# A three-part kernel on one core: weight conversions in other steps of the MLP loop, and four small copies earlier

## The chip, the cores and the metric

The kernel runs on one core of a Trainium2 chip. The metric is the time of one execution on the device in microseconds (us), lower being better. The times are medians over repeated runs; the profile is of one execution.

## What is computed

Attention with two kinds of mask, a soft mixture of experts, and an MLP, one after the other. The change lies in the MLP and its input:

```python
c = logits - logits.max(1, keepdims=True)      # 2304 tokens x 32 slots
c = np.exp(c)
c /= c.sum(1, keepdims=True) + 1e-09
x = c @ slot_out                               # 2304 x 512
h = np.maximum(x @ w_in, 0.0)                  # w_in 512 x 2048
out = h * h @ w_out                            # w_out 2048 x 512
```

All weights arrive as 64-bit floats.

## The kernel before

Attention and experts take the first 200 us. The MLP never forms `x`. It computes A = slot_out @ w_in in quarters of 512 columns (`a_chunk`, line 1090), and h as c @ A.

**The loop.** The 2048 hidden columns are taken in NC = 4 quarters c, the tokens in NSB = 3 blocks of 768, and the 4 pieces of 128 hidden columns of a quarter are the innermost loop (QF = 4). That makes 48 steps n, 12 for each quarter, and j is the step's number in its quarter. A step multiplies one piece of h (768 tokens x 128) by one 128 x 512 piece of w_out: 18 matmuls on PE (line 1205), three for each of six token tiles t, into six PSUM banks, named `s`, `s`, `o`, `o`, `t1`, `t1`. The three are high part of h by high part of the weight, low part of h by high, high by low: the third one needs the weight's low half.

After four steps (j = 3, 7, 11) the banks are full and are emptied into `part`: in the first quarter by copies, one bank on ACT and the next on DVE (line 1218), in the others by additions on DVE alone (line 1220). In the last quarter each result is sent out.

**h.** `emit_h` (line 1155) makes half a piece of h, some one and a half steps ahead: one PE matmul (line 1165) into a bank `t2`, relu and square on ACT (1173, 1174), rounding to the high part on ACT (1175), the low part by a subtraction on DVE (1180). It is called twice in a step, at t = 1 and t = 4.

**Conversions.** `conv_late` (1084) takes the next loaded weight piece and makes 32-bit values of it (`narrow`, 178): one instruction on POOL (line 189, into `nm`), then three on DVE (192, 193, 196, the last into `wi` for w_in or `wf` for w_out). For w_out two more follow one step later in `conv_split` (at t = 1): a rounding on ACT to the high half (1081) and a subtraction on POOL to the low half (1082). The order is fixed: w_out 0 to 3, then for each of quarters 1, 2 and 3 four pieces of w_in and four of w_out. Each conversion frees the buffer of its 64-bit piece, and `fetch` issues the next load into it on SP's queue. Two w_out pieces are converted ahead of the loop, the rest at t = 4 of a step, where the line of the diff allows it: before, steps 0 to 9 of the first quarter, and j = 2 to 9 of the second and third.

**Combine weights.** c (2304 x 32) is kept as high and low part. `c_parts` (978) copies the two parts of one of the four batches side by side (POOL, lines 981 and 982, tile `c4`, two buffers), and `c_transpose` (984) transposes them on PE (line 990) into `cT4`, the moving operand of line 1165. Batches 0 and 1 are copied during the experts, three groups of transposes run ahead of the loop, and five behind steps 0, 1, 3, 4 and 5 (`TR`).

**Order.** The program order of each of the four compute engines is pinned as the code emits it; an engine takes its instructions in that order, and each waits for what it needs.

Of the kernel before, what the change touches and what calls it, by code (L numbers as in the profile page):

```python
# [31 lines left out]
def kernel(  # L32
# [49 lines left out]
    def behind(ins, other):  # L82

        tc.add_manual_dep(
            ins.ins, other.ins.name,
            mybir.DependencyInfo(mybir.DependencyClass.NoSync, mybir.DependencyReason.DATA),
            reason="issue order",
        )
# [32 lines left out]
    def psum(tag):  # L121
        if tag == "t":
            tag = ("t1", "t1", "t2", "t2")[nt[0] % 4]
            nt[0] += 1
        return pp.tile([128, 512], F32, tag=tag, name=tag, bufs=2)


    def fill(n, ins):
        ps = psum("s")
        for _ in range(n):  # L130
            new = nc.tensor.matmul(
                out=ps[:, 0:256], lhsT=identb, rhs=fillb, start=True, stop=True
            )
            behind(new, ins)
            ins = new
# [821 lines left out]
    def c_softmax():  # L957
        cm = tail.tile([128, NTT], F32, name="cm")
        ch = tail.tile([128, NTT, 32], F32R, name="ch")
        behind(nc.vector.tensor_reduce(out=cm, in_=cl_, axis=AX.X, op=ALU.max), sT_ready)  # L960
        nc.vector.tensor_tensor(
            out=cl_, in0=cl_, in1=cm[:, :, None].to_broadcast([128, NTT, 32]), op=ALU.subtract
        )
        nc.scalar.activation(out=cl_, in_=cl_, func=AF.Exp)
        nc.vector.tensor_reduce(out=cm, in_=cl_, axis=AX.X, op=ALU.add)
        nc.vector.tensor_scalar(out=cm, in0=cm, scalar1=1e-9, scalar2=None, op0=ALU.add)
        nc.vector.reciprocal(out=cm, in_=cm)
        nc.vector.tensor_tensor(
            out=cl_, in0=cl_, in1=cm[:, :, None].to_broadcast([128, NTT, 32]), op=ALU.mult
        )  # L970
        nc.scalar.copy(out=ch, in_=cl_)
        chf = ch.bitcast(F32)
        nc.vector.tensor_tensor(out=cl_, in0=cl_, in1=chf, op=ALU.subtract)
        return chf
# [3 lines left out]
    def c_parts(chf, b):  # L978

        c4 = c4s[b] = tail.tile([128, 5, 2, 32], F32, tag="c4", name="c4", bufs=2)  # L980
        nc.gpsimd.tensor_copy(c4[:, :, 0, :], chf[:, 5 * b:5 * b + 5, :])
        nc.gpsimd.tensor_copy(c4[:, :, 1, :], cl_[:, 5 * b:5 * b + 5, :])

    def c_transpose(b, t0, t1, after=None):
        c4 = c4s[b]
        ps = psum("t2")
        n = min(t1 * 128, S) - t0 * 128
        for t in range(t0, t1):
            nr = min(128, S - t * 128)
            ins = nc.tensor.transpose(  # L990
                out=ps[0:64, ts(t - t0, 128)][:, 0:nr], in_=c4[0:nr, t].rearrange("p a s -> p (a s)"),
                identity=ident[0:nr, 0:nr],
            )
            if after is not None:
                behind(ins, after)
            after = None
        c0 = b * S + t0 * 128
        for i in range(2):
            (nc.vector.tensor_copy if i else nc.scalar.copy)(out=cT4[ts(i, 64), c0:c0 + n], in_=ps[0:64, 0:n])
        return ins  # L1000
# [76 lines left out]
    def conv_split():  # L1077
        while split:
            t, r = split.pop(0)
            hi, lo = t[:, 0:512], t[:, 512:1024]  # L1080
            nc.scalar.copy(out=hi, in_=r)  # L1081
            nc.gpsimd.tensor_tensor(out=lo, in0=r, in1=hi.bitcast(F32), op=ALU.subtract)  # L1082

    def conv_late(early=False):
        if todo or early:
            (conv_in if todo[0][0] == "in" else lambda: conv_out(early))()
            fetch()


    def a_chunk(c, tag, n0=0, n1=2):  # L1090
        two = tag == "o"
        pss = [psum(tag)[:, 0:(n1 - n0) * 128] for _ in range(1 + two)]
        for n in range(n0, n1):
            for kt in range(KD):
                for i in range(2):
                    ins = nc.tensor.matmul(
                        out=pss[i * two][ts(i, 64), ts(n - n0, 128)],
                        lhsT=soT[:, kt].rearrange("p a s -> p (a s)"),
                        rhs=wi[c][kt][:, ts(2 * n + i, 128)],
                        start=(kt == 0), stop=(kt == KD - 1), tile_position=(0, 64 * i),  # L1100
                    )
        if c == 0 and n0 == 0:
            fill(6, ins)
        if n0 == 0:
            A4[c] = mp.tile([128, 512], F32R, tag="A4", name="A4", bufs=2)
        cv = A4[c].rearrange("p (s i w) -> p i s w", i=2, w=128)[:, :, n0:n1]
        pv = [p.rearrange("p (s w) -> p s w", w=128) for p in pss]
        for i in range(2):
            nc.scalar.copy(out=cv[0:64, i], in_=pv[i * two][ts(i, 64)])
        for i in range(2):  # L1110
            nc.vector.tensor_tensor(
                out=cv[64:128, i], in0=pv[i * two][ts(i, 64)], in1=cv[0:64, i].bitcast(F32), op=ALU.subtract
            )

    CP = [(b, t0, t1) for b in range(B) for t0, t1 in ((0, 3), (3, 5))]
    for layer, pr in order:
# [5 lines left out]
        if (layer, pr) == (2, 0):  # L1122
            chf = c_softmax()
# [13 lines left out]
    A4 = {}  # L1137
    conv_split()
    a_chunk(0, "o", 0, 1)


    TB = 6
# [2 lines left out]
    QF = KF // NC  # L1145
    seq = [(c, sb, QF * c + j) for c in range(NC) for sb in range(NSB) for j in range(QF)]
    gs = {}

    TR = (0, 1, 3, 4, 5)


    halves = [(n, i) for n in range(len(seq)) for i in range(2)]
# [2 lines left out]
    def emit_h():  # L1155
        if not halves:
            return
        n, i = halves.pop()
        c, sb, f = seq[n]
        if i == 0:  # L1160
            gs[n] = slot(F32R), slot(F32R)
        gh, gl = (x[:, ts(i, HB)] for x in gs[n])
        ps = psum("t2")
        c0 = sb * 2 * HB + i * HB
        nc.tensor.matmul(  # L1165
            out=ps[:, 0:HB], lhsT=A4[c][:, ts(f % QF, 128)], rhs=cT4[:, c0:c0 + HB], start=True, stop=True
        )
        r = mp.tile([128, HB], F32, tag="r", name="r", bufs=3)
        if n == 0 and i:
            nc.vector.tensor_scalar(out=r, in0=ps[:, 0:HB], scalar1=0.0, scalar2=None, op0=ALU.max)  # L1170
            nc.vector.tensor_tensor(out=r, in0=r, in1=r, op=ALU.mult)
        else:
            nc.scalar.activation(out=r, in_=ps[:, 0:HB], func=AF.Relu)  # L1173
            nc.scalar.activation(out=r, in_=r, func=AF.Square)  # L1174
        nc.scalar.copy(out=gh, in_=r)  # L1175
        lows.append((gl, r, gh))
        if n or i:
            while lows:
                gl, r, gh = lows.pop(0)
                nc.vector.tensor_tensor(out=gl, in0=r, in1=gh.bitcast(F32), op=ALU.subtract)  # L1180
# [8 lines left out]
    for n, (c, sb, f) in enumerate(seq):  # L1189
        gh, gl = gs.pop(n)  # L1190
        first, last = f % QF == 0, f % QF == QF - 1
        j = n % (NSB * QF)
        if first:
            acc = [psum(a) for a in ("s", "s", "o", "o", "t1", "t1")]
        for t in range(TB):
            if t == 1:
                emit_h()
                conv_split()
            elif t == 4:
                emit_h()  # L1200

                if n < QF - 2 or QF - 2 <= j < 3 * QF - 2:
                    conv_late()
            for k, (a, w) in enumerate(((gh, 0), (gl, 0), (gh, 1))):
                nc.tensor.matmul(  # L1205
                    out=acc[t], lhsT=a[:, ts(t, 128)], rhs=wo[f][:, ts(w, 512)],
                    start=(first and k == 0), stop=(last and k == 2),
                )
            if not last:
                continue  # L1210

            r = sb * TB + t
            pt = part[:, r]
            nh = 2 if n == len(seq) - 1 and t == TB - 1 else 1
            for i in range(nh):
                cs = ts(i, 512 // nh)
                if c == 0:
                    (nc.vector.tensor_copy if t % 2 else nc.scalar.copy)(out=pt, in_=acc[t])
                else:
                    nc.vector.tensor_tensor(out=pt[:, cs], in0=acc[t][:, cs], in1=pt[:, cs], op=ALU.add)  # L1220
                if c == NC - 1:
                    nc.sync.dma_start(out=out[128 * r:128 * r + 128, cs], in_=pt[:, cs])
        if j == 3 * QF - 4 and c < NC - 1:
            a_chunk(c + 1, "t2")
        if n in TR:
            x = CP[3 + TR.index(n)]
            if x[1] == 0:
                c_parts(chf, x[0])
            c_transpose(*x)
    pin()  # L1230


# [28 lines left out]
```

## Time and profile before

| | |
|---|---|
| median of 3 runs | 446.71 us (443.96 to 447.89) |
| span of the profiled execution | 439.8 us |
| PE busy (matmul) | 411.3 us, 94% |
| DVE, ACT, POOL busy | 260.4, 282.3, 63.4 us |
| MLP loop on PE, first to last matmul | 203.2 us to 435.3 us |
| HBM read, written | 64.55 MB, 4.72 MB |

The span is the time from the first to the last instruction of the profiled execution; no time of that execution beside its span is shown, and the median of the runs is 6.9 us above it. The profile gives for each engine its instructions with start and duration, and for idle time what ended it.

### The profile page before, as it was taken

To read this page: it belongs to the slowest core of one execution; us is meant where nothing else is said; L and a number is where in the kernel's file an instruction comes from. 1 tells how busy PE (TensorE), PEld (TensorE's weight loads), DVE (VectorE), ACT (ScalarE), POOL (GpSimd) and SP (SyncE) were. 2 spreads that over 40 slices of the span, in tenths; PEclk is the share of its full clock that TensorE was granted. 3 is DMA by queue.
4 is the path that set the end of the run, shared out by engine and by line. 5 is a ranking of instruction groups with operands and counts; after the bars stand their busy time and mean duration, and the time that the engine had idled before them with its cause. 6 is when DMAs were issued, how large, how long until landed. Compare 5 with 4: busy or idle time off the path is not lost.

```text
span 439.8 us, 8657 instructions
## 1 busy us (share of the span) xinstructions
PE 411.3 (94%) x3310; PEld 305.6 (69%) x3310; DVE 260.4 (59%) x577; ACT 282.3 (64%) x583; POOL 63.4 (14%) x91
## 2 busy tenths in 40 slices
PE   8987988999989899979799999999999999999995
PEld 5665665766757644446578788877888787888884
DVE  7485665765766651036676754678664777725444
ACT  5977667887767411016686787657666676766660
POOL 7211001010110001002440340012320113100000
PEclk9998989999989969999999999999999999999999
DMA  9998939769957889998233211412000000003033
GB/s 193 284 280 246 253 93 302 219 195 281 323 165 230 283 309 371 386 401 327 95 95 97 97 43 54 136 56 95 1 1 1 0 0 2 0 1 144 24 121 144
DMA packets 38889, 69.83 MB, mean 159 GB/s; under 512 B 12736, under 2 KB 19136, under 8 KB 38848
## 3 DMA queue, kind: packets, MB, share of 16 engines
q1 hardware_dynamic: 38848, 69.28, 50.3%
q8 instruction: 26, 0.43, 0.4%
q14 instruction: 15, 0.12, 0.1%
HBM read 64.55 MB, written 4.72 MB: 158 GB/s over the span
## 4 chain that ended last, share of the span: by engine, by line
PE 67%; ACT 12%; DVE 10%; issue 5%; DMA 3%; POOL 1%; SPq 0%; DVEq 0%; ACTq 0%; POOLq 0%
PE t L1205 12%; PE s L1205 12%; PE o L1205 11%; PE s L532 4%; PE o L1010 4%; ACT space L471 3%; ACT space L477 3%; PE s L508 3%; PE t L452 3%; PE t L1037 3%; DVE part L1220 3%; PE t L1165 3%; DMA w<-in_moe_w_in_dram 2%; PE o L613 2%; DVE nm L193 2%
## 5 line engine op out<-in xcount | busy, mean ns | idle before, releaser
L1180 DVE TENSOR_TENSOR w<-r,w 128x384 fp32r<-128x384 f32 x96 | 57.8, 606 | 82.5 <-ACT w L1175 82.2
L1205 PE MATMUL s<-w 128*128 128x512 f32 x288 | 83.0, 396 | 0.5 <-POOL w L1082 0.5
L1205 PE MATMUL t<-w 128*128 128x512 f32 x288 | 75.1, 395 | 3.6 <-DVE part L1220 3.5
L1173 ACT ACTIVATE r<-t 128x384 f32<-128x384 f32 x95 | 46.7, 491 | 46.1 <-PE t L1165 38.7
L1205 PE MATMUL o<-w 128*128 128x512 f32 x288 | 73.7, 391 | 0.0
L1205 PEld LDWEIGHTS t<-w 128*128 128x128 f32 x288 | 53.0, 188 | 15.6 <-DVE part L1220 5.0
L1205 PEld LDWEIGHTS o<-w 128*128 128x128 f32 x288 | 54.0, 188 | 12.4
L1205 PEld LDWEIGHTS s<-w 128*128 128x128 f32 x288 | 52.7, 188 | 11.3 <-POOL w L1082 0.9
L1174 ACT ACTIVATE r<-r 128x384 f32<-128x384 f32 x95 | 50.0, 526 | 3.0
L1175 ACT CAST w<-r 128x384 fp32r<-128x384 f32 x96 | 49.2, 514 | 3.3
L471 ACT COPY space<-t 64x288 f32<-64x288 f32 x62 | 38.0, 614 | 11.7 <-PE t L452 10.3
L452 PE MATMUL t<-ident,space 96*128 96x96 f32 x192 | 29.7, 283 | 3.9 <-ACT space L477 2.3
L189 POOL TENSOR_SCALAR nm<-w 128x512 f32<-128x512 f32 x28 | 20.0, 720 | 90.5 <-DVE w L196 35.2
L1082 POOL TENSOR_TENSOR w<-wf,w 128x512 fp32r<-128x512 f32 x16 | 21.2, 1325 | 78.6 <-ACT w L1081 78.6
L1165 PE MATMUL t<-cT,A 128*128 128x384 f32 x96 | 32.2, 337 | 0.0
L477 ACT ACTIVATE space<-t 64x288 f32<-64x288 f32 (+1 forms) x46 | 29.0, 642 | 3.2 <-PE t L452 2.1
L452 PEld LDWEIGHTS t<-ident,space 96*128 96x128 f32 x192 | 20.6, 157 | 12.3 <-issue 3.9
L551 POOL TENSOR_TENSOR space<-space,sm 128x576 f32<-128x576 f32 x7 | 8.3, 1191 | 100.7 <-DVE sm L550 29.9
L193 DVE SCALAR_TENSOR_TENSOR nm<-w,nm 128x512 uint32<-128x512 uint32 x32 | 22.1, 692 | 1.0
L532 PE MATMUL s<-space 128*36 128x72 f32 x256 | 22.2, 317 | 0.0
L485 DVE TENSOR_REDUCE mx<-s 128x8 f32<-128x288 f32 (+2 forms) x32 | 14.9, 469 | 12.3 <-PE s L532 6.8
L1165 PEld LDWEIGHTS t<-cT,A 128*128 128x128 f32 x96 | 17.9, 188 | 4.4 <-ACT r L1173 0.5
(189 smaller groups left out, 564.5 us busy)
## 6 DMA issues: line engine op xcount, KB each, us to landing
w<-in_moe_w_dram SPq DMA_DIRECT2D x47, 512.0 KB
space<-in_moe_w_dram SPq DMA_DIRECT2D x17, 512.0 KB
w<-in_moe_w_in_dram SPq DMA_DIRECT2D x16, 512.0 KB
w<-in_moe_w_out_dram SPq DMA_DIRECT2D x16, 512.0 KB
space<-in_k_dram SPq DMA_DIRECT2D x16, 288.0 KB
space<-in_q_dram SPq DMA_DIRECT2D x16, 288.0 KB
out_dram<-part SPq DMA_DIRECT2D x17, 256.0 KB
space<-in_v_dram SPq DMA_DIRECT2D x16, 144.0 KB
```

The source lines that it names most:

```text
L193: nc.vector.scalar_tensor_tensor(out=r, in0=hi, scalar=0x80000000, in1=r, op0=ALU.bitwise_and, op1=ALU.bitwise_or)
L452: nc.tensor.transpose(out=pv[:, r, :], in_=src[:, h, 2 * r:2 * r + 2, :], identity=ident[0:96, 0:96])
L471: ins = (nc.vector.tensor_copy if dve else nc.scalar.copy)(out=o, in_=i)
L477: nc.scalar.activation(out=o, in_=i, func=AF.Copy, scale=scale)
L532: nc.tensor.matmul(out=ps[64 * h:64 * h + 36, ts(r, 72)].rearrange("p (a w) -> p a w", a=2), lhsT=qv[:, h, 4 * g + r, :], rhs=kv[:, :, h, ...
L1082: nc.gpsimd.tensor_tensor(out=lo, in0=r, in1=hi.bitcast(F32), op=ALU.subtract)
L1165: nc.tensor.matmul(out=ps[:, 0:HB], lhsT=A4[c][:, ts(f % QF, 128)], rhs=cT4[:, c0:c0 + HB], start=True, stop=True)
L1173: nc.scalar.activation(out=r, in_=ps[:, 0:HB], func=AF.Relu)
L1174: nc.scalar.activation(out=r, in_=r, func=AF.Square)
L1175: nc.scalar.copy(out=gh, in_=r)
L1180: nc.vector.tensor_tensor(out=gl, in0=r, in1=gh.bitcast(F32), op=ALU.subtract)
L1205: nc.tensor.matmul(out=acc[t], lhsT=a[:, ts(t, 128)], rhs=wo[f][:, ts(w, 512)], start=(first and k == 0), stop=(last and k == 2),)
```

## The change

Two edits, both in the MLP. The table `CONV` takes the place of the range j = 2 to 9: conversions now run in steps j = 1, 2, 4, 5, 6, 8, 9, 10 of a quarter (and still in steps 0 and 1), not in 3, 7 and 11, the steps that empty the banks. There are eight places in a quarter as before, but the first quarter now has 9 and had 10, so that the last piece of each later group moves to j = 1 of the next quarter. And the copies of batch 2 are issued right behind the first `a_chunk` ahead of the loop instead of behind step 1; those of batch 3 behind step 1 instead of behind step 4.

```diff
@@ -1137,6 +1137,7 @@
     A4 = {}
     conv_split()
     a_chunk(0, "o", 0, 1)
+    c_parts(chf, 2)
@@ -1147,6 +1148,7 @@
     TR = (0, 1, 3, 4, 5)
+    CONV = [j for j in range(1, 3 * QF - 1) if j % QF != QF - 1]
@@ -1199,7 +1201,7 @@
             elif t == 4:
                 emit_h()
 
-                if n < QF - 2 or QF - 2 <= j < 3 * QF - 2:
+                if n < QF - 2 or j in CONV:
                     conv_late()
@@ -1223,10 +1225,9 @@
         if n in TR:
-            x = CP[3 + TR.index(n)]
-            if x[1] == 0:
-                c_parts(chf, x[0])
-            c_transpose(*x)
+            c_transpose(*CP[3 + TR.index(n)])
+            if n == 1:
+                c_parts(chf, 3)
     pin()
```

Two lines are added ahead of the loop's body, so its line numbers rise by two (1205 becomes 1207, 1220 becomes 1222).

DVE's order around step 15, which empties the banks of the second quarter's first block, before. `part` with an `s`, `o` or `t1` bank is an addition, `w<-r,w` is the low part of h, and lines 192, 193 and 196 are one conversion:

```order
L196 SCALAR_TENSOR_TENSOR wi_3393<-w_2841,nm_3394 128x512
L1220 TENSOR_TENSOR part_2622<-s_3291,part_2622 128x512
L1180 TENSOR_TENSOR w_3385<-r_3413,w_3384 128x384
L1220 TENSOR_TENSOR part_2622<-s_3292,part_2622 128x512
L1220 TENSOR_TENSOR part_2622<-o_3293,part_2622 128x512
L1220 TENSOR_TENSOR part_2622<-o_3294,part_2622 128x512
L1180 TENSOR_TENSOR w_3431<-r_3434,w_3430 128x384
L192 TENSOR_SCALAR nm_3439<-nm_3439 128x512
L193 SCALAR_TENSOR_TENSOR nm_3439<-w_2886,nm_3439 128x512
L196 SCALAR_TENSOR_TENSOR wi_3393<-w_2886,nm_3439 128x512
L1220 TENSOR_TENSOR part_2622<-t1_3295,part_2622 128x512
L1220 TENSOR_TENSOR part_2622<-t1_3296,part_2622 128x512
```

And the same place in the changed kernel:

```order
L196 SCALAR_TENSOR_TENSOR wi_3393<-w_2844,nm_3394 128x512
L1222 TENSOR_TENSOR part_2622<-s_3280,part_2622 128x512
L1182 TENSOR_TENSOR w_3385<-r_3413,w_3384 128x384
L1222 TENSOR_TENSOR part_2622<-s_3281,part_2622 128x512
L1222 TENSOR_TENSOR part_2622<-o_3282,part_2622 128x512
L1222 TENSOR_TENSOR part_2622<-o_3283,part_2622 128x512
L1182 TENSOR_TENSOR w_3431<-r_3434,w_3430 128x384
L1222 TENSOR_TENSOR part_2622<-t1_3284,part_2622 128x512
L1222 TENSOR_TENSOR part_2622<-t1_3285,part_2622 128x512
L1182 TENSOR_TENSOR w_3431<-r_3458,w_3430 128x384
```

The conversion that stood between the fourth and the fifth addition has moved to the next step; the one ahead of the first addition is where it was.

POOL's order from the first weight's low half (ahead of the loop) to the fourth weight's, before. Line 189 begins a conversion, line 1082 is a low half, and `c_2795` is the tile of batch 2:

```order
L1082 TENSOR_TENSOR w<-wf,w 128x512
L189 TENSOR_SCALAR nm<-w 128x512
L1082 TENSOR_TENSOR w<-wf,w 128x512
L189 TENSOR_SCALAR nm<-w 128x512
L1082 TENSOR_TENSOR w<-wf,w 128x512
L189 TENSOR_SCALAR nm<-w 128x512
L981 COPY c_2795<-ch 128x5x32
L982 COPY c_2795<-lN 128x5x32
L1082 TENSOR_TENSOR w<-wf,w 128x512
```

And in the changed kernel, where `c_2647` is batch 2 and `c_2804` batch 3:

```order
L1082 TENSOR_TENSOR w<-wf,w 128x512
L981 COPY c_2647<-ch 128x5x32
L982 COPY c_2647<-lN 128x5x32
L189 TENSOR_SCALAR nm<-w 128x512
L1082 TENSOR_TENSOR w<-wf,w 128x512
L189 TENSOR_SCALAR nm<-w 128x512
L1082 TENSOR_TENSOR w<-wf,w 128x512
L189 TENSOR_SCALAR nm<-w 128x512
L981 COPY c_2804<-ch 128x5x32
L982 COPY c_2804<-lN 128x5x32
L1082 TENSOR_TENSOR w<-wf,w 128x512
```

Batch 2's copies have moved ahead of three conversions, and batch 3's stand where batch 2's were.

## Rows read from the trace of the kernel before

**Rows 1.** The page's costliest groups: busy us, mean ns, idle before.
```profile
L1205 PE MATMUL t<-w 128*128 128x512 f32 x288 | 75.1, 395 | 3.6 <-DVE part L1220 3.5
```

**Rows 2.** Waits of PE, 190 to 440 us: us in total, times, longest.
```profile
PE t L1205 <- DVE part L1220: 3.5, 4, 0.9
PE t L990 <- POOL c L982: 2.3, 1, 2.3
```

**Rows 3.** Windows of steps: busy us of each engine, granted clock, DMA share, GB/s.
```profile
256.55:261.03 4.48, 4.48 (x21) 3.72 (x20) 2.83 (x5) 3.48 (x7) 1.54 (x3) 1.00 0.00 2
283.43:289.09 5.66, 4.76 (x22) 3.66 (x20) 5.59 (x12) 3.51 (x7) 0.65 (x1) 1.00 0.26 93
302.56:310.17 7.61, 6.74 (x53) 5.20 (x52) 7.51 (x13) 4.09 (x8) 3.44 (x4) 1.00 0.20 71
245.06:251.91 6.85, 6.74 (x54) 5.18 (x52) 4.84 (x9) 4.91 (x10) 3.08 (x4) 1.00 0.29 103
```

**Rows 4.** Timeline of DVE, steps 15 and 16: start us, us, instruction [idle before].
```profile
279.39 0.56 DVE L1180 TENSOR_TENSOR w<-r,w 128x384 fp32r<-128x384 f32 x1 [1.68 <-ACT w L1175]
279.86 0.42 DVE L192 TENSOR_SCALAR nm<-nm 128x512 uint32<-128x512 uint32 x1
...
281.04 0.69 DVE L196 SCALAR_TENSOR_TENSOR wi<-w,nm 128x512 uint32<-128x512 uint32 x1
...
285.06 0.41 DVE L192 TENSOR_SCALAR nm<-nm 128x512 uint32<-128x512 uint32 x1
...
286.85 1.28 DVE L1220 TENSOR_TENSOR part<-t,part 128x512 f32<-128x512 f32 x2
```

**Rows 5.** Timeline of PE, steps 15 and 16.
```profile
282.04 1.55 PE L1205 MATMUL t<-w 128*128 128x512 f32 x6
...
286.35 0.33 PE L1165 MATMUL t<-cT,A 128*128 128x384 f32 x1
287.58 1.67 PE L1205 MATMUL t<-w 128*128 128x512 f32 x6 [0.90 <-DVE part L1220]
```

**Rows 6.** Timeline of ACT, POOL and PE, end of step 22.
```profile
317.73 0.62 ACT L1081 CAST w<-wf 128x512 fp32r<-128x512 f32 x1 [0.30 <-DVE wf L196]
...
318.44 1.29 POOL L1082 TENSOR_TENSOR w<-wf,w 128x512 fp32r<-128x512 f32 x1 [2.98 <-ACT w L1081]
...
319.26 0.84 PE L1205 MATMUL s<-w 128*128 128x512 f32 x3
```

**Rows 7.** Timeline of POOL, DVE and PE, end of step 1.
```profile
214.68 0.63 POOL L189 TENSOR_SCALAR nm<-w 128x512 f32<-128x512 f32 x1
214.77 0.95 DVE L1180 TENSOR_TENSOR w<-r,w 128x384 fp32r<-128x384 f32 x1 [1.21 <-ACT w L1175]
215.27 0.64 POOL L981 COPY c<-ch 128x160 f32<-128x160 f32 x1
...
215.85 0.51 POOL L982 COPY c<-lN 128x160 f32<-128x160 f32 x1
...
216.41 0.52 PE L990 MATMUL t<-ident,c 128*64 128x128 f32 x3 [2.27 <-POOL c L982]
...
216.69 0.95 PE L1205 MATMUL s<-w 128*128 128x512 f32 x3
216.94 0.69 DVE L196 SCALAR_TENSOR_TENSOR wf<-w,nm 128x512 uint32<-128x512 uint32 x1
```

**Rows 8.** Timeline of POOL and DVE, conversion of weight 1.
```profile
199.64 0.65 POOL L189 TENSOR_SCALAR nm<-w 128x512 f32<-128x512 f32 x1
...
205.88 0.42 DVE L192 TENSOR_SCALAR nm<-nm 128x512 uint32<-128x512 uint32 x1
```

**Rows 9.** Timeline of PE, step 1 and end of step 8.
```profile
209.83 0.50 PE L1205 MATMUL s<-w 128*128 128x512 f32 x1 [0.50 <-POOL w L1082]
210.16 0.33 PE L1165 MATMUL t<-cT,A 128*128 128x384 f32 x1
...
248.15 1.93 PE L1205 MATMUL t<-w 128*128 128x512 f32 x6
```

## The prediction, made before the changed kernel's time was known

> **What bounds the kernel now.** I began with the page's costliest groups: the MLP loop's matmuls (line 1205) on PE, 0.40 us each and overlapping, with almost no idle time before them; for tile `t` it is 3.6 us in all, put down to DVE's additions into `part` (line 1220) [rows 1]. So PE is the bound of the loop, and an edit of DVE or POOL work can give back no more than PE's pauses. The waits of PE list these: four for a bank, 3.5 us together, and one of 2.3 us for POOL's copies `c` [rows 2].
>
> A pause costs a little more than the wait shown, so next I measured whole steps [rows 3]. I number the loop's 48 steps n = 0 to 47, j = n mod 12; a step is 18 matmuls of line 1205 and starts with those of the first `s` bank: step 8 at 245.06, 16 at 283.43, 20 at 302.56. An undisturbed step takes 4.48 us. Step 16 takes 5.66, so its pause costs 1.18. Step 20 carries the 32 small matmuls of `a_chunk` too and takes 7.61; step 8 has the same 32 and takes 6.85, of which 0.38 is a pause of its own (its `t` group takes 1.93 [rows 9], the same group of step 15 takes 1.55 [rows 5]). So step 20 loses 7.61 - (6.85 - 0.38) = 1.14. The granted clock is 1.00 in these rows, the higher level (2.4 GHz).
>
> Why step 16 pauses is read from DVE [rows 4]. Step 15 starts at 278.95 (283.43 - 4.48). A conversion is three DVE instructions (lines 192, 193, 196). The one that the code places in step 14 starts at 279.86, that is 0.91 into step 15: on DVE a conversion runs about a step after its place in the code. It ends at 281.73, and the six banks are emptied behind it. Step 15's own conversion starts at 285.06, ahead of the last two banks, `t`. Their additions start at 286.85, the first ends at about 287.53, and PE, whose matmul ahead of that bank starts at 286.35, goes on at 287.58 after a wait of 0.90 [rows 5].
>
> **The change part by part.**
>
> *Conversions leave the emptying steps 3, 7, 15, 19, 27, 31.* In DVE's order step 15's conversion is gone from ahead of the `t` additions; step 14's stays in its place. So the `t` additions start where the conversion did, at 285.06 instead of 286.85, and end at 285.74 and 286.34. PE wants these banks from about 286.35 on, the second some 0.7 later: 0.6 us to spare. The pauses should go. Steps 16, 20, 28 and 32 give 1.18 + 1.14 + 1.18 + 1.14 = 4.64; the waits of [rows 2] alone would say 3.5, which is the lower bound. Step 8, behind step 7, gives its 0.38.
>
> *Conversions come into steps 10, 13, 22, 25, 34, 37.* Those of 10, 22 and 34 run on DVE inside the emptying steps 11, 23 and 35. That is one conversion ahead of the additions, as step 15 is left with, so I cost it at nothing, with 0.3 (half of the spare time) as upper bound for each. ACT's rounding (line 1081) and POOL's low half (line 1082) of a weight follow a step later and move with it; they are behind one another in the same order as before. SP's loads keep their order too: each follows a conversion that frees a buffer, many steps ahead of its own conversion, which hides the step or two by which they move. If one were late, POOL's line 189 would wait for it, and behind it DVE.
>
> *One weight of each quarter comes later.* The last output weight of quarters 1 to 3 is now converted at j = 1 (steps 13, 25, 37) and wanted two steps on. Such a conversion, in a step without additions, is that of step 21 [rows 6]: ACT rounds at 317.73, POOL makes the low half from 318.44 to 319.73. Step 23 starts at 319.26: ready 0.47 into the step that would want it. It is wanted by the third matmul, 0.45 in (0.84 - 0.39). Step 1 shows what a late low half costs beside the wait [rows 9]: the matmul starts at 209.83 and the next group only at 210.16, 0.33 later, where matmuls that flow follow each other at 0.23 (half of 0.45). So 0.05 late and 0.1 for the restart: 0.15 each, 0.45 for three. Bounds: 0 and 0.3 each.
>
> *The copies `c_parts(2)` move ahead of the loop.* PE's transposes waited for them, 0.64 + 0.51 us on POOL, until 216.41 [rows 7]. With them made early the transposes start at 214.14. What is late next is the low half of weight 3, wanted in step 3. Its conversion does not move, since `c_parts(3)` takes the very place that `c_parts(2)` leaves: DVE's line 196 still ends at 217.63. ACT and POOL need 2.0 us from there (317.73 to 319.73), so it is ready at about 219.7. Step 2 now starts at 214.42 and takes 4.59 (4.48, and 0.95 for its first group instead of 0.84): step 3 starts at 219.01 and wants it at 219.46. With the restart 0.36 is given back, 1.91 stays. At their new place the copies push back POOL's line 189 of weight 1 by their 1.15; it ended at 200.29, and DVE takes it up at 205.88 [rows 8], which hides it.
>
> *POOL beside DVE.* Line 1180 takes 0.56 alone [rows 4] and 0.95 where it starts just behind POOL's line 189 [rows 7]. Two places come to that. The moved copies may stand beside the two subtractions of line 1111 ahead of the loop, which PE waits for: 0 to 2 x 0.39 = 0.78. I take 0, as those read a bank and one operand from SBUF, where line 1180 reads two from SBUF. And in steps 15 and 27 POOL's low half ends 0.47 in, so its next line 189 meets line 1180, which starts 0.44 in (279.39): 0.39 of the 0.6 to spare is gone and 0.2 is left. I take no loss, with 0.3 a step as bound.
> The Trainium skill ("SBUF — State Buffer", section "Who interferes with whom") has a rule for this: a DVE instruction with two SBUF inputs shares a port with GpSimd, and the one that starts second is blocked for the other's whole length; with one SBUF input there is no contention. The 0.95 row agrees, as line 1180 started 0.09 behind POOL's 0.63 and ended 0.41 after it. By the rule line 1111 loses nothing, and without it the sum below would be lower by up to 0.78.
>
> Sum: 4.64 + 0.38 + 1.91 - 0.45 = 6.48. The profiled execution's span is 439.8, so 433.3 after. The median of the runs shown is 446.71, 6.9 above that span, a distance that I keep: **440.2 us**, 0.985 of before. All costs at their lower bound: 4.64 + 0.38 + 2.27 = 7.3, 439.4. All at their upper: 3.5 + 0.38 + 1.91 - 0.9 - 0.78 - 5 x 0.3 = 2.6, 444.1.
>
> **The rivals.**
>
> *R1, one conversion is still too many.* For: DVE's time to spare is 0.6, and 0.2 in steps 15 and 27. Against: in step 15 the additions of `s` and `o`, which already stand behind one conversion only, made no wait of PE [rows 2]. If the four pauses stay half as long, 2.3 of the 6.48 is lost: 4.2, 442.5.
>
> *R2, the change does not do what it says.* DVE lags the code by a step, so leaving out j = 3 and 7 may only change which conversion stands among the additions. For: step 14's does run in step 15. Against: the order, where it stands ahead of all six and the late one is gone. Then only the copies gain: 446.71 - 1.91 = 444.8.
>
> *R3, slower.* The conversions at j = 1 have the least room, 0.47 against 0.45. POOL's line 189 for each of these weights is queued behind the low half of the weight before. If that pushed the conversion on by a whole step, PE would wait 4.48 in steps 15, 27 and 39: 13.4 - 6.9 = 6.5 slower, 453.2. It decides from 2.3 us of delay each on (three times that is the 6.9 gained elsewhere). Against: in the order line 189 of that weight stands ahead of the conversion by two steps, and DVE has no additions in steps 14, 26 and 38.
>
> **How the numbers follow.** Forecast (a gain of 5 to 7.5) 0.68, R1 0.16, R2 0.11, R3 0.05. The forecast's own range is 439.2 to 441.7. The runs shown lie 3.9 us apart (443.96 to 447.89), so I let the whole range begin 1.4 lower, at 437.8, and end at 444.5, just above the case of all upper bounds; R3 and most of R2 stay out. About 1% (4.5 us) is what a measurement of this kernel can tell from no change, and the forecast is only 2 us beyond it: faster by over 1% in nine of ten of the forecast's cases and a third of R1's, 0.67; slower by over 1% in R3, 0.04; within, 0.29.
>
> **What would show it.** After the change PE should wait for no addition (line 1222 by its new number) and for no `c`. Steps 16 and 28 should take 4.5 us, 20 and 32 6.5, step 2 should start 2.3 us earlier against step 1. Waits for POOL's low halves should stand in steps 1, 3 and, short, in 15, 27 and 39. In step 15 the last addition should end before 286.9 less what was gained until then. The forecast is wrong if PE waits over 0.3 us for an addition in steps 12, 16, 24, 28 or 36, or over 0.5 for POOL in steps 15, 27 and 39, or if line 1111 takes twice as long.

## The result and the profile after

The changed kernel takes 437.85 us (median of 20 runs, 435.30 to 442.92); the kernel before took 445.12 us beside it (20 runs, 439.53 to 448.96). The ratio is 0.9885, with a 95% interval of 0.9855 to 0.9916; it is nearer to 1 than that of the two medians because it leaves disturbed runs out. 440.2 us had been predicted, in a range of 437.8 to 444.5.

The profiled execution has a span of 436.1 us, and its time was 437.79: 1.7 us lie around a span. Its page, line 1207 with the `s` banks and with tile `t` (busy us, mean ns | idle before):

```profile
L1207 PE MATMUL s<-w 128*128 128x512 f32 x288 | 83.7, 398 | 1.0 <-POOL w L1082 1.0
...
L1207 PE MATMUL t<-w 128*128 128x512 f32 x288 | 74.4, 393 | 0.0
```

The 3.6 us ahead of tile `t` [rows 1] are gone. The waits of PE from 190 to 440 us, and of its weight loads PEld, which are a list of their own (us in total, times, longest):

```profile
PE t L1037 <- DMA w<-in_moe_w_dram: 1.5, 3, 0.7
PE o L1053 <- DVE so L1045: 1.4, 1, 1.4
PE s L1207 <- POOL w L1082: 1.0, 2, 0.5
PE t L1096 <- ACT r L1175: 0.3, 1, 0.3
...
PEld s L1207 <- POOL w L1082: 2.7, 6, 0.9
...
PEld s L1207 <- DVE part L1222: 0.4, 2, 0.2
```

Neither the additions nor `c` stand in PE's list [rows 2]; two waits for POOL's low halves do, and two short ones for an addition stand only in that of PEld. What this is worth is read from whole steps, here 1, 3, 8, 16 and 20 (columns as in [rows 3]: start and end, length, busy us of PE, PEld, DVE, ACT and POOL with the number of instructions, granted clock, DMA share, GB/s):

```profile
211.09:216.71 5.62, 5.12 (x24) 3.92 (x24) 3.50 (x6) 4.53 (x10) 2.68 (x3) 1.00 0.30 93
221.41:227.02 5.61, 5.11 (x23) 3.67 (x21) 4.08 (x7) 4.65 (x10) 3.50 (x4) 1.00 0.06 11
245.94:252.41 6.47, 6.47 (x53) 5.26 (x52) 3.51 (x7) 4.01 (x8) 0.00 (x0) 1.00 0.32 110
283.97:288.61 4.64, 4.64 (x21) 3.60 (x20) 4.14 (x8) 3.07 (x7) 0.00 (x0) 1.00 0.39 117
302.08:308.56 6.48, 6.48 (x54) 5.26 (x52) 4.83 (x9) 3.47 (x7) 0.00 (x0) 1.00 0.16 40
```

Against [rows 3], step 16 falls from 5.66 to 4.64, 20 from 7.61 to 6.48 and 8 from 6.85 to 6.47. Every step, from the starts of their first `s` matmul in the timeline of PE, in us:

```
step          before  after   gain      forecast
1              8.10    5.62   2.48       2.27
2 and 3        9.45   10.31  -0.86      -0.36
8              6.85    6.47   0.38       0.38
16             5.66    4.64   1.02       1.18
20             7.61    6.48   1.13       1.14
28             5.66    4.62   1.04       1.18
32             7.57    6.47   1.10       1.14
15, 27, 39    13.44   13.65  -0.21      -0.45
all others                    0.07       0
steps 0 to 45 223.56  217.41  6.15       6.48
```

From step 0 to step 46 the loop takes 6.15 us less in these two profiles. The span shrank by 3.7 only, since step 0 started at 205.67 instead of 203.17. Part of that 2.5 us is earlier than anything the change touches; 1.4 lie just ahead of the loop. The timeline of PE after, and its window from 200 to 204 us:

```profile
199.17 0.66 PE L1053 MATMUL o<-same,so 128*128 128x64 f32 x4 [1.41 <-DVE so L1045]
199.66 0.60 PE L131 MATMUL s<-ident,identb 128*128 128x256 bf16 x4
200.19 1.87 PE L1096 MATMUL o<-wi,soT 128*64 128x128 f32 x16
```

```profile
200.00:204.00 4.00, 4.00 (x27) 2.75 (x24) 0.73 (x3) 0.70 (x3) 1.92 (x4) 0.57 1.04 412
```

The granted clock is 0.57 there, near the lower level (1.2 GHz), and the 16 matmuls of `a_chunk` take 1.87 us. Whether the moved copies cause this is taken up at the end of the experiments.

### The profile page after: what moved, and what is told of

Same layout as the page of the kernel before. It is cut to its first block, busy times and chain, and to the rows that moved or that the text cites. A ratio compares the mean times of both kernels' runs of the same rounds, so it can differ in the third digit from the quotient of the medians.

```text
span 436.1 us, 8653 instructions
## 1 busy us (share of the span) xinstructions
PE 411.6 (94%) x3310; PEld 307.0 (70%) x3310; DVE 259.0 (59%) x577; ACT 282.2 (65%) x583; POOL 64.0 (15%) x91
## 4 chain that ended last, share of the span: by engine, by line
PE 71%; ACT 10%; DMA 8%; issue 5%; DVE 3%; POOL 1%; DVEq 0%; ACTq 0%; POOLq 0%; SPq 0%
PE s L1207 14%; PE t L1207 14%; PE o L1207 14%; DMA w<-in_moe_w_dram 7%; PE s L532 4%; PE s L508 4%; PE t L452 4%; ACT space L477 4%; ACT space L471 4%; PE t L1167 3%; PE o L613 2%; DMA w<-in_moe_w_in_dram 2%; PE t L582 2%; PE o L783 2%; PE t L1096 1%
## 5 line engine op out<-in xcount | busy, mean ns | idle before, releaser
L1182 DVE TENSOR_TENSOR w<-r,w 128x384 fp32r<-128x384 f32 x96 | 56.0, 584 | 77.1 <-ACT w L1177 76.9
```

## The experiments

Three theories were to be told apart. **A**, the prediction's: additions come late through what stands ahead of them on DVE, low halves through the place of their conversion in DVE's order. **B**: a low half that is late holds up what comes behind it, on POOL or through PE's own pause. **C**, for the loop's start: the copies issued early slow the head of the loop. Steps and loop times are read as in the table above; "the loop" is step 0 to step 46. What A and B come to at a place, its expectation says.

### The two edits apart

Conversions alone (the copies' calls are where they were; this edit and the others here are shown against the changed kernel):

```diff
-    c_parts(chf, 2)
...
-            c_transpose(*CP[3 + TR.index(n)])
-            if n == 1:
-                c_parts(chf, 3)
+            x = CP[3 + TR.index(n)]
+            if x[1] == 0:
+                c_parts(chf, x[0])
+            c_transpose(*x)
```

> The conversions of the change alone; the copies of batches 2 and 3 stay where they were. My theory (a conversion ahead of the last two additions makes PE's bank pauses, the copies make the pause at the end of step 1, and both are separate): step 1 takes 8.1 us as before, step 3 about 4.85, step 8 6.47, steps 16, 20, 28, 32 take 4.6, 6.5, 4.6, 6.5, and the loop from step 0 to step 46 takes 223.6 - 4.6 = 219.0. Rival (the copies at their new place set the head of the loop back): the loop starts 4.5 us or less after the last second-layer matmul of the experts, as before, and at full clock, where the changed kernel took 1.4 longer. Time 441 to 442 if before is 446.

Copies alone:

```diff
-                if n < QF - 2 or j in CONV:
+                if n < QF - 2 or QF - 2 <= j < 3 * QF - 2:
```

> The copies alone at their new place; conversions as before. My theory: step 1 takes 5.6 instead of 8.1, step 3 5.6 instead of 4.85, step 2 0.1 more; the four bank pauses stay (5.66 and 7.6), step 8 keeps 6.85; the loop from step 0 to step 46 takes 223.6 - 1.6 = 222.0, the time is lower by 1 to 2 us, not to be told from before. Rival (the moved copies slow the head): the stretch from the last second-layer matmul to step 0 is 1.4 longer than before and nothing is gained.

Conversions alone: 440.39 us, 0.9944 of the kernel before (0.9903 to 0.9986), loop 220.51. Copies alone: 441.78 us, 0.9969 (0.9925 to 1.0013), loop 221.82. The second is as expected: steps 1 to 3 as in the changed kernel (5.59, 4.71, 5.62), the four pauses as before, 1.74 us gained in the loop, though its time is not to be told from that of the kernel before. The first gained 3.05 where 4.6 was expected (219.0). Steps 16, 20, 28 and 32 took 4.67, 6.48, 4.63 and 6.47; what was missing lies in steps 1 and 2 (8.31 and 5.80, before 8.10 and 4.60). Its windows of these two steps and PE's timeline at their border:

```profile
210.98:219.29 8.31, 5.56 (x25) 4.00 (x24) 5.61 (x9) 5.03 (x11) 4.81 (x6) 0.95 0.40 119
219.29:225.09 5.80, 5.80 (x23) 4.75 (x22) 1.80 (x3) 3.65 (x8) 1.62 (x2) 0.77 0.03 11
```

```profile
218.79 0.85 PE L990 MATMUL t<-ident,c 128*64 128x128 f32 x3 [2.26 <-POOL c L982]
219.29 1.63 PE L1206 MATMUL s<-w 128*128 128x512 f32 x3
```

Behind the wait of 2.26 us the granted clock fell, 0.77 on average over step 2, and three matmuls took 1.63 us that take 0.95 in the kernel before [rows 7] behind the same wait. This cost 0.21 + 1.20 = 1.41 us in this execution; without it the conversions give 3.05 + 1.41 = 4.46, and 4.46 + 1.74 = 6.20 is the changed kernel's 6.15. So the two edits add up, each is worth about what the table gives it, and the wait that the copies take away may cost more than its own length.

### Where a conversion stands, not in which step

Here the steps of before come back (j = 2 to 9), with the copies early, but in an emptying step the conversion is issued behind the last addition:

```diff
-    CONV = [j for j in range(1, 3 * QF - 1) if j % QF != QF - 1]
+    CONV = range(QF - 2, 3 * QF - 2)
...
-                if n < QF - 2 or j in CONV:
+                if (n < QF - 2 or j in CONV) and not last:
...
+        if last and j in CONV:
+            conv_late()
```

> The copies as in the changed kernel, conversions in the same steps as before (j = 2 to 9), but in the emptying steps 3, 7, 15, 19, 27, 31 issued behind the step's last addition and not at t = 4. If the place ahead of the last two additions makes the pauses, and not the number of conversions in these steps, steps 16, 20, 28, 32 take 4.5 and 6.5 as in the changed kernel, and steps 15, 27, 39 take 4.48. If a conversion beside the emptying costs wherever it stands, part of the 1.1 comes back in steps 16, 20, 28, 32.

Loop 216.93, steps 15, 16, 27, 28 and 39 all 4.48, 20 and 32 6.47 and 6.48; 439.5 us in one run. Its timeline of DVE in steps 15 and 16, the last two additions and what follows:

```profile
287.72 1.27 DVE L1222 TENSOR_TENSOR part<-t,part 128x512 f32<-128x512 f32 x2
288.92 0.41 DVE L192 TENSOR_SCALAR nm<-nm 128x512 uint32<-128x512 uint32 x1
```

The emptying step converts again, and no pause is left. With the same copies and the same steps, but the conversion at t = 4, the copies alone kept the pauses (5.64 and 7.62 in steps 16 and 20). So the pauses came from the conversion's place ahead of the last two additions, as A has it [rows 4], and leaving the step out of the table is one way to move it. With the conversions in the old steps no weight comes late either, so this loop is 0.48 shorter than that of the changed kernel.

### What is left in steps 15, 16, 27 and 28

In the changed kernel step 16 takes 4.64, not 4.48. Its timelines of DVE, POOL and PEld, steps 15 (from 279.42) and 16 (from 283.97):

```profile
279.90 0.88 DVE L1182 TENSOR_TENSOR w<-r,w 128x384 fp32r<-128x384 f32 x1 [1.71 <-ACT w L1177]
280.71 0.87 DVE L192 TENSOR_SCALAR nm<-nm 128x512 uint32<-128x512 uint32 x1
...
284.11 0.68 DVE L1222 TENSOR_TENSOR part<-s,part 128x512 f32<-128x512 f32 x1
...
278.46 1.30 POOL L1082 TENSOR_TENSOR w<-wf,w 128x512 fp32r<-128x512 f32 x1 [11.02 <-ACT w L1081]
279.73 1.57 POOL L189 TENSOR_SCALAR nm<-w 128x512 f32<-128x512 f32 x2
...
279.82 0.19 PEld L1207 LDWEIGHTS s<-w 128*128 128x128 f32 x1 [0.20 <-POOL w L1082]
...
284.84 0.53 PEld L1207 LDWEIGHTS s<-w 128*128 128x128 f32 x3 [0.21 <-DVE part L1222]
```

The weight load of the third matmul waits 0.20 for the late low half, and step 15 loses 0.07. Behind the low half POOL starts line 189 twice, and beside them line 1182 takes 0.88 instead of 0.56 and line 192 takes 0.87 instead of 0.42 [rows 4]: 0.77 us more on DVE, so that the second `s` addition ends at 284.79, 0.82 into step 16, and a weight load waits 0.21 for it. First the late conversion was moved one step forward, to j = 0, so that its low half is in time:

```diff
-    CONV = [j for j in range(1, 3 * QF - 1) if j % QF != QF - 1]
+    CONV = [0] + [j for j in range(2, 3 * QF - 1) if j % QF != QF - 1]
```

> The changed kernel with the last weight of each quarter converted at j = 0 instead of j = 1. If the 0.07 that steps 15, 27, 39 lose and the 0.16 and 0.14 of steps 16 and 28 come from that one late conversion (low half late, and POOL's next line 189 beside DVE's line 1182 ahead of the additions), all five take 4.48. If the 0.15 in steps 16 and 28 comes from the one conversion that is still ahead of the additions, they stay at 4.62 to 4.64.

433.11 us in one run, loop 216.93, steps 15, 16, 27, 28 and 39 at 4.48. The timelines of DVE and PEld in step 15 (from 275.25) and at the start of step 16 (279.73):

```profile
275.69 0.56 DVE L1182 TENSOR_TENSOR w<-r,w 128x384 fp32r<-128x384 f32 x1 [1.68 <-ACT w L1177]
276.16 0.42 DVE L192 TENSOR_SCALAR nm<-nm 128x512 uint32<-128x512 uint32 x1
...
279.10 0.68 DVE L1222 TENSOR_TENSOR part<-s,part 128x512 f32<-128x512 f32 x1
...
280.41 0.59 PEld L1207 LDWEIGHTS s<-w 128*128 128x128 f32 x3
```

Here the same addition ends at 279.78, 0.05 into step 16 and 0.63 ahead of the weight load that uses its bank. But this takes away the late low half and POOL's meeting with DVE in one go. So, on top of this, the meeting was put back alone, as three copies on POOL into a spare tile `scr`, whose result nothing uses:

```diff
                 nc.vector.tensor_tensor(out=gl, in0=r, in1=gh.bitcast(F32), op=ALU.subtract)
+                if n in (16, 28) and i == 0:
+                    for k in range(3):
+                        nc.gpsimd.tensor_copy(scr, gh.bitcast(F32))
```

> The version with the late conversion at j = 0 (no late low half, steps 15, 16, 27 and 28 at 4.48 us) plus three POOL copies of 384 columns, about 1.5 us, issued so that they start with line 1182 in steps 15 and 27; their results are used by nothing. Theory A (the rest of 0.16 in steps 16 and 28 of the changed kernel is POOL's work beside DVE): line 1182 there takes about 0.9 instead of 0.56 and line 192 longer than 0.42, the additions come 0.5 to 0.8 later, steps 16 and 28 take 4.55 to 4.7. Theory B (it was the late low half itself, through PE's pause in steps 15 and 27): steps 15, 16, 27 and 28 stay at 4.48.

This run did not answer the question. Step 15 took 6.20 and step 16 4.83, loop 221.02 (440.0 us in one run), for a reason of its own. Timelines of DVE, POOL and PE:

```profile
278.48 0.56 DVE L1182 TENSOR_TENSOR w<-r,w 128x384 fp32r<-128x384 f32 x1 [1.68 <-ACT w L1177]
281.19 0.85 DVE L192 TENSOR_SCALAR nm<-nm 128x512 uint32<-128x512 uint32 x1 [2.15 <-POOL nm L189]
...
278.51 2.03 POOL L1185 COPY scr<-w 128x384 f32<-128x384 f32 x3 [4.47 <-ACT w L1177]
...
284.24 0.94 PE L1211 MATMUL s<-w 128*128 128x512 f32 x3 [1.55 <-DVE part L1226]
```

The copies stood on POOL ahead of the line 189 that the conversion in step 15 needed, DVE waited 2.15 us for it with six additions queued behind, and PE waited 1.55. Line 1182 itself, which started 0.03 us ahead of the copies, kept its 0.56. In the next run four such copies stand behind that line 189, again on top of `e3_j0`:

```diff
                 if n < QF - 2 or j in CONV:
                     conv_late()
+                if n in (14, 26):
+                    for k in range(4):
+                        nc.gpsimd.tensor_copy(scr, gs[n + 2][0][:, 0:HB].bitcast(F32))
```

> As f4_meet, but with four POOL copies of 384 columns issued behind step 14's and step 26's own conversion instead of ahead of it, so that they hold up no line 189 that these steps need. They start with the low part of h in steps 15 and 27 and lie beside lines 192, 193 and 196. Theory A (POOL's work beside DVE delays the additions): the three conversion instructions take 0.3 to 0.8 us longer together, the additions come later by as much, step 15 stays at 4.48, step 16 takes 4.5 to 4.7. Theory B (only the late low half and PE's pause did it): DVE may stretch, but steps 15, 16, 27 and 28 stay at 4.48.

440.57 us in one run. Steps 15 and 27 take 4.48, steps 16 and 28 4.78. Timelines of DVE, POOL and PEld, step 15 from 282.15, step 16 from 286.63:

```profile
283.07 0.73 DVE L192 TENSOR_SCALAR nm<-nm 128x512 uint32<-128x512 uint32 x1
283.83 0.88 DVE L193 SCALAR_TENSOR_TENSOR nm<-w,nm 128x512 uint32<-128x512 uint32 x1
284.74 0.87 DVE L196 SCALAR_TENSOR_TENSOR wi<-w,nm 128x512 uint32<-128x512 uint32 x1
...
286.14 0.88 DVE L1182 TENSOR_TENSOR w<-r,w 128x384 fp32r<-128x384 f32 x1
...
282.62 3.36 POOL L1209 COPY scr<-w 128x384 f32<-128x384 f32 x4 [3.87 <-ACT w L1177]
...
287.67 0.53 PEld L1211 LDWEIGHTS s<-w 128*128 128x128 f32 x3 [0.39 <-DVE part L1226]
```

With no low half late, a conversion beside POOL's copies takes 0.73 + 0.88 + 0.87 = 2.48 us instead of 0.42 + 0.69 + 0.69 = 1.80, 0.68 more. The copies also push POOL's own two lines 189 back beside the second line 1182, which takes 0.88 where it takes 0.62 in `e3_j0`. With both, the second `s` addition ends 0.99 into step 16 instead of 0.05, and the step loses 0.30, somewhat more than the 4.5 to 4.7 expected. So A holds: POOL's work beside DVE is enough. That the late low half matters in steps 16 and 28 because it lets line 189 start beside line 1182 is read from the changed kernel's timeline; no run changed that alone.

### Steps 1 to 3

Steps 1 and 3 each lose 0.76 to a low half (an undisturbed step with transposes behind it takes 4.86). After, timelines of PE, DVE and POOL at the start of step 3 (221.41):

```profile
219.47 0.69 DVE L196 SCALAR_TENSOR_TENSOR wf<-w,nm 128x512 uint32<-128x512 uint32 x1
...
222.53 0.50 PE L1207 MATMUL s<-w 128*128 128x512 f32 x1 [0.51 <-POOL w L1082]
...
220.77 0.56 DVE L1182 TENSOR_TENSOR w<-r,w 128x384 fp32r<-128x384 f32 x1
...
220.90 1.58 POOL L1082 TENSOR_TENSOR w<-wf,w 128x512 fp32r<-128x512 f32 x1 [2.02 <-ACT w L1081]
```

The low half takes 1.58 us beside line 1182, where it takes 1.29 alone [rows 6]. Three runs of one edit each: the conversion of weight 1 ahead of the third half of h,

```diff
-    emit_h()
     conv_late()
+    emit_h()
```

> The changed kernel with one line moved: ahead of the loop the conversion of weight 1 is issued before the third half of h instead of behind it. Theory A (steps 1 and 3 each wait for a low half of their own, late by its place in DVE's queue): the conversion's first DVE instruction (line 192) starts about 1.3 us earlier against step 0, step 1 falls from 5.62 to about 4.86 us with no wait for POOL, step 3 stays at 5.6, the loop from step 0 to step 46 goes from 217.41 to about 216.6. Theory B (one late chain of low halves, weight 1's passes its delay on to weights 2 and 3 through POOL's order): steps 1, 2 and 3 all shorten, loop about 215.9. Nothing changes behind step 4 by either.

the conversions of steps 0 and 1 at t = 2,

```diff
+            elif t == 2 and n < QF - 2:
+                conv_late()
...
-                if n < QF - 2 or j in CONV:
+                if n >= QF - 2 and j in CONV:
```

> The changed kernel with the conversions of steps 0 and 1 (weights 2 and 3) issued at t = 2 instead of t = 4, so that on DVE they stand ahead of the second low part of h of their step. Theory A (place in DVE's queue): weight 3's low half ends 1 us or more earlier against the start of step 3, step 3 falls from 5.61 to about 4.85 and step 2 by 0.1; step 1 stays at 5.62; loop 216.5. Theory B (POOL's low half of 1.58 us and the copies of batch 3 on POOL make step 3's loss): the low half stays beside the same DVE instruction and step 3 keeps more than half of its 0.76, loop above 217.0.

and the copies of batch 3 behind step 3 instead of step 1:

```diff
-            if n == 1:
+            if n == 3:
```

> The changed kernel with the copies of batch 3 behind step 3 instead of behind step 1. Theory A (weight 3's low half is late by its conversion's place in DVE's queue and by line 1182 beside it): step 3 stays within 0.15 us of 5.61, step 2 of 4.70. Theory B (the 1.1 us of copies on POOL make it late): step 3 falls to 5.2 or less. Steps 4 and 5 stay at 4.86 and 4.96 unless the transposes of batch 3, which follow step 4, come to wait for them.

```
              step 1  step 2  step 3   loop    time of one run
changed        5.62    4.70    5.61   217.41
f1_w1          4.87    4.59    5.47   216.47   440.55
f2_t2          5.62    4.59    5.01   216.79   437.16
f8_c3_later    5.63    4.68    5.52   217.23   440.56
```

The first removes step 1's loss and 0.14 of step 3's; the second most of step 3's, 0.16 short of what was expected; later copies on POOL bring 0.09. (In seven profiles in which nothing ahead of step 3 differs, it takes 5.59 to 5.67.) Step 3 follows the place of its conversion in DVE's order, as A says, and little else. A small share is handed on from step 1, as B has it: with weight 1 earlier, steps 2 and 3 are 0.11 and 0.14 shorter.

### The moves together

Weight 1 earlier, t = 2 in steps 0 and 1, and j = 0 instead of 1, the three edits shown above in one kernel; twice, the second time beside the changed kernel itself on the same chip:

> Three moves together on the changed kernel: weight 1's conversion ahead of the third half of h, the conversions of steps 0 and 1 at t = 2, and the late conversion of each quarter at j = 0 instead of j = 1. If the remaining losses are independent: steps 1 and 3 4.86 each, steps 15, 16, 27, 28 and 39 4.48, loop 217.41 - 0.76 - 0.86 - 0.48 = 215.3, that is 2.1 us less than the changed kernel and 8.2 less than the kernel before, a ratio of 0.981 to the kernel before. If they are not (an earlier conversion pushes a low part of h late): a wait of PE for a w of DVE in steps 1 to 3, loop above 216.2, ratio above 0.984.

> The same kernel as f3_best again, beside the changed kernel on one chip. The steps as there (loop from step 0 to step 46 215.3 us). If the loop alone differs: 2.1 us less than the changed kernel, 8.2 less than the kernel before, ratio 0.981. If the start of the loop, which came between 201.5 and 209.4 us in ten profiles, hides it: a ratio between 0.981 and 0.99, with an interval that reaches the changed kernel's.

> The changed kernel itself again, on the same chip as f6_best. Loop from step 0 to step 46 217.4 us again, whatever the time at which step 0 starts; ratio to the kernel before 0.986 if only the loop's 6.15 us counts, 0.9885 if the first comparison is repeated. If moving the copies slowed the head of the loop (start of step 0 against the last expert matmul later by over 1 us than before), it does so again in this profile; if that was this execution's granted clock, it does not.

The loop takes 215.30 and 215.28 us, as the sum of the single gains had it (217.41 - 0.94 - 0.62 - 0.48 = 215.37). Steps 1, 2 and 3 take 4.87, 4.59 and 4.87, and no wait for a low half is left in PE's list; step 1 begins without one:

```profile
209.96 0.97 PE L1209 MATMUL s<-w 128*128 128x512 f32 x3
210.77 0.34 PE L1167 MATMUL t<-cT,A 128*128 128x384 f32 x1
```

Times: 437.2 us (6 runs, 430.90 to 438.34), 0.9823 of the kernel before (0.9733 to 0.9912), and 431.26 us (7 runs, 428.38 to 437.12), 0.9675 (0.9613 to 0.9738; the two medians, 431.26 and 443.57, give 0.972). The changed kernel beside the second: 438.99 us (6 runs, 434.00 to 440.46), 0.9865 (0.9806 to 0.9923), loop 217.38. So this version beats the kernel before in both comparisons, and the changed kernel in the second, beside it; the interval of the first still holds the changed kernel's 0.9885. That 8.3 us of the loop show as 1.8% once and 3.3% the other time is not of the loop, which is the same to 0.02 us in both.

### Where the loop starts

Over all 14 profiles step 0 starts between 201.45 and 209.39 us, and these starts do not follow the edits: `e3_j0` and `e4_behind`, which differ in nothing ahead of the loop, have 201.45 and 207.81. Two windows of unchanged stages, first in the trace of the copies alone (step 0 at 207.34), then in that of `e3_j0`:

```profile
10.00:20.00 10.00, 9.52 (x94) 6.86 (x94) 3.78 (x9) 9.39 (x17) 3.79 (x12) 0.59 1.09 255
160.00:170.00 10.00, 10.00 (x56) 5.03 (x60) 4.91 (x9) 1.73 (x3) 0.72 (x1) 0.58 0.64 227
```

```profile
10.00:20.00 10.00, 9.36 (x94) 6.55 (x90) 3.77 (x9) 9.55 (x18) 3.78 (x12) 1.00 1.10 264
160.00:170.00 10.00, 10.00 (x92) 3.39 (x84) 3.81 (x7) 3.06 (x5) 1.70 (x4) 1.00 0.97 337
```

The clock granted differs between executions of the same stages, 0.58 against 1.00. In the first window this shows no cost, 94 matmuls in both. In the second the two executions have not come equally far, so its 56 and 92 matmuls are not the same ones. The same eight matmuls a little ahead of it take, first in the trace of the copies alone (granted clock 0.50 from 159.7 to 161.5), then in that of `e3_j0` (1.00 from 156.3 to 157.3):

```profile
159.78 1.91 PE L930 MATMUL s<-dz,utot 128*128 128x32 f32 x8
156.37 1.08 PE L930 MATMUL s<-dz,utot 128*128 128x32 f32 x8
```

As to theory C, the way from PE's wait of 1.41 us for `so` to step 0 takes 5.10 to 5.11 us or 6.35 to 6.52, nothing between. It is the long one in six profiles, all with early copies (the changed kernel twice, `f2_t2`, `f3_best`, `f6_best`, `f8_c3_later`), and the short one in six others with the same early copies, and in the two without. In `e3_j0`:

```profile
196.35 0.66 PE L1053 MATMUL o<-same,so 128*128 128x64 f32 x4 [1.41 <-DVE so L1045]
196.84 0.60 PE L131 MATMUL s<-ident,identb 128*128 128x256 bf16 x4
197.37 1.10 PE L1096 MATMUL o<-wi,soT 128*64 128x128 f32 x16
```

The same wait, the same copies, and 1.10 us instead of 1.87. So early copies do not bring it about by themselves. What differs is the granted clock: on this way it is 0.73 to 0.74 on average in the six long cases and 1.00 in the eight short ones, and at 1.00 the way is as long with the early copies as without. By their expectations the copies alone (5.11) speak against C and the second profile of the changed kernel (6.41) for it. Two profiles without them are too few to say that they have no part in it; this stays open.

## Why the prediction came out as it did

**What bounds the kernel, and the four pauses: right.** PE is the bound, the conversion ahead of the last two additions was the cause (`e4_behind`), and rival R1 (one conversion still too many) falls: steps 12, 24 and 36, whose conversions came into the emptying steps before them, took 4.46 to 4.48. Of 4.64 us, 4.29 came. The step that failed is "POOL beside DVE", where 0.39 of the 0.6 to spare was counted and no loss taken: line 1182 lost 0.32, the second line 189 stretches line 192 too, by 0.45, and 0.77 is more than 0.6. The 0.6 had been worked out for the `t` additions, and the wait came earlier, at the second `s` addition, which happens to have as much to spare (0.63 in `e3_j0`). The bound of 0.3 a step held the 0.16 and 0.14 that were lost, and none of the signs of a wrong forecast came: the longest wait for an addition is the 0.21 of a weight load. The Trainium skill ("SBUF — State Buffer", section "Who interferes with whom") names the case in a clause that the prediction left out: an instruction with one SBUF input contends as well if it runs in a mode that uses both ports, and it names `tensor_scalar`, the operation of line 192, among those that can. The row of 0.87 agrees, though no row tells by itself that line 192 runs in such a mode. That the instruction which starts first is not held up agrees too: line 1182 kept 0.56 with POOL 0.03 behind it.

**The copies: right in kind, two terms mis-sized.** The terms are the 2.27 that step 1 was to gain and the 0.36 to be given back. Step 1 gave 2.48, not 2.27; as with a pause for a bank, the step lost more than the wait. Against it, steps 2 and 3 lost 0.86, not 0.36. Line 196 of weight 3 ended where it was put, at 220.16 (217.63, and 2.5 for the later start). Two things behind it were off and make up the 0.40 that step 3 lost beyond the forecast: the low half took 1.58, not 1.29, and step 3 started 0.1 earlier than worked out. Step 2 lost 0.10 with its first group, where the weight load waits 0.27 for a low half, a wait that was not foreseen. The term of line 1111, put at nothing, is nothing: its two places take 0.61 and 0.59 us in both kernels. The moved copies had ended before it began (at 201.30 and 202.36), so this does not test the rule on one SBUF input.

**The late low halves: right, and smaller.** 0.07 each instead of 0.15. The low half was ready earlier than worked out, 0.34 into step 15 and not 0.47, but it is wanted by the weight load, some 0.2 into the step, and not by the third matmul at 0.45. The weight load waited 0.20, and only 0.07 of it reached the matmuls. R3 (slower) did not come near, and R2 (only the copies gain) falls with the conversions' 4.46.

**Step 8:** 0.38, as read.

**From the loop to the time: right by luck in part.** 437.85 us lies 0.05 inside the range that was given (437.8 to 444.5) and outside the forecast's own (439.2 to 441.7); what holds it is the 1.4 by which the range was begun lower for the scatter of the runs. The forecast kept 6.9 us between the profiled span and the median. Only 1.7 of it is fixed; the other 5.2 is the distance of that one execution from a median of three, which is itself 1.6 above that of 20. Where the other executions of the kernel before spend that time is not shown, since only one was profiled: its loop began early (203.17), and its wait for `c` left the clock at 1.00, where the same wait cost `e1_conv_only` 1.41. Over 20 runs the median of before is 445.12, and 445.12 - 6.15 = 438.97 is 1.1 above the time measured. As a ratio, 440.2 of 446.71 is 0.985, and the two comparisons gave 0.9885 and 0.9865. The 6.15 us of the loop are 1.4% of 445.12.

## What to carry over

An engine that takes its work in order delivers late whatever stands behind a long job, so ask for each result that the bounding engine waits for what stands ahead of it in that order: moving a conversion behind the last addition of the same step gave as much as moving it to another step. Spare time on such an engine has to be counted with every instruction that a neighbour can stretch, and the list of waits of the weight loads read beside that of the matmuls, since pauses that cost 0.07 to 0.30 us a step showed only there. And where the code ahead of a stage varies by more between executions than the change can give, measure the stage from its first to its last instruction: 215.30 and 215.28 us say more than medians of 437.2 and 431.26.

## What the runs showed of the hardware

- A DVE instruction with one input (line 192, 0.42 us) took 0.87 beside line 189 of POOL and 0.73 beside POOL's copies; with two inputs (lines 193, 196) 0.88 and 0.87 instead of 0.69. It works the other way too: POOL's low half took 1.58 instead of 1.29 beside line 1182, which had started ahead of it and kept its 0.56.
- A weight load waits for its weight or its bank by itself. It is some 0.2 us ahead of its matmul (in `e3_j0` the weight loads of step 15 begin at 275.02, the step at 275.25), so that a result is wanted that much earlier than the matmul's start says.
- Behind one and the same wait of PE (2.27 us for `c`) the granted clock stayed at 1.00 in the kernel before and fell in the kernel with the conversions alone, where it cost 1.41 us more. Behind the wait of 1.41 us for `so` it fell in six of 14 executions, at a cost of 1.2 to 1.4 us each.
